# Batch 0's B and C loaded eight tokens to a partition, scaled and transposed in that layout

## The chip, the cores and the metric

The kernel runs on one core of a Trainium2 chip. The metric is the device time of one execution in microseconds (us). Engines are named as the profile names them: PE (matrix products; PEld are its weight loads), DVE (vector), ACT (activations and copies), POOL, and SP, whose queue here issues every transfer between memory and the chip.

## The reference, cut to what matters

A Mamba-2 scan over chunks feeds a low-rank mixer with a channel network. All sizes are small: 4 batches, 8 heads, 768 tokens, 32 values and 16 states per head.

```python
log_a = np.log(np.clip(a, 1e-06, 1.0))
for c in range(nc):                              # chunks of 32 tokens
    xc, Bc, Cc = (x[:, :, sl], B[:, :, sl], C[:, :, sl])
    cum = np.cumsum(log_a[:, :, sl], axis=-1)
    L = np.exp(cum[:, :, :, None] - cum[:, :, None, :]) * causal
    y_intra = ((Cc @ Bc^T) * L) @ xc
    y_inter = (Cc @ state) * np.exp(cum)[..., None]
    y[:, :, sl] = y_intra + y_inter
    state = np.exp(sum(la)) * state + (Bc * np.exp(cum[..., -1:] - cum)[..., None])^T @ xc
...
# y, with heads side by side: X (4, 768, 256)
h = (X.transpose(0, 2, 1) @ U) @ V               # over all 768 tokens, rank 32
u = X + h.transpose(0, 2, 1)
out = u + np.maximum(u @ w_ch1, 0.0) @ w_ch2
```

The four weight arrays arrive as 64-bit floats and are made into 32-bit ones on the chip.

## The kernel before

The kernel takes tokens in chunks of 64. Twelve *pairs* k = 0 to 11 (three to a batch) each cover 256 tokens: two blocks of 128 tokens, or four chunks. Instead of the reference's L it scales B by exp(-sum) and C by exp(+sum), where the sum of log a runs from the middle of each chunk; the array F holds both factors, by tokens.

Everything stands in an order written out by hand: LOADS names the loads issued before anything else, and PLAN is a list of steps that the function `follow` turns into instructions. Each engine takes its instructions strictly in that order. The letters that matter here, k being the pair:

- `b`k.part, `x`k.block, `B`, `X`, `L`: loads of B (two parts, 0 and 2), C (part 1) and x. All go through `begin` (L184) into SP's queue. `Z`/`z` load V and U, `W`/`w` the channel weights.
- `A`, `K`: `decays` and `keep`, the factors F and the decay between chunks.
- `P` (and `Q` for a part): `prep`, DVE scales a pair's B and C by F into BC, by tokens (tokens on partitions).
- `T` (and `V` for one block): `turning` (L478 to L491), PE transposes BC so that states lie on partitions, and ACT (or DVE) copies the result into T and into Cm (C once for even and once for odd heads).
- `g`: `gram` (L509), C times B for all chunks; `m`, `M`: `mask` on DVE; `s`: `state` (L541), B times x; `u`: `update`, DVE carries the state through the chunks, then POOL makes Sm (L567).
- `i`, `j`: `inter` in two halves (L611), `n`: `intra` (L633), `y`: copies of the output (L646), `t`, `O`: transposes of it by tokens (L654).
- `c`: conversion of a piece of the 64-bit weights (DVE and ACT, L415 to L422); `v`: `spread`, V for the mixer (L820, L824); `R`: `refine`, splits of the weights.
- `p`, `q`: the mixer's projection on U (L681, L689); `a`: its product with V added to yT (L699); `U`: the first product of the channel network for batch 0 (L727, with ACT's L744); `d`: the second one; `S`, `f`, `e`, `h` do the same in three parts for batches 1 to 3.
- `F`: products with the identity that write nothing used, to keep PE busy (L137).

Batch 0's mixer needs all of batch 0's scan, pairs 0 to 2, since `p` sums over all tokens. The scan of pair 3 and part of 4 runs in among it. From the first `U` on PE has large products to fill it.

The head of the two lists reads so (LOADS, then the start of PLAN):

```python
'b0.0 b0.1 b0.2 x0.0 x0.1 b1.0 b1.1 b1.2 '
'x1.1 F2.0 A0 Q0.1 x1.0 Q0.0 F3.1 b2.2 A1 Q0.2 V0.1.1 Q1.2 V0.0.0 K0 Q1.1 g0 m0 Q1.0 s0 V1.1.2 '
'M0 n0 u0 V1.0.2 b3.0 F1.1 Q2.1 s1 u1 i0 g1 m1 F3.0 M1 b2.0 Q2.0 b2.1 Q2.2 F1.0 j0 y0 Z0 V2.0.2 '
```

A B load of one block is 128 partitions x 8 heads x 16 floats, 1024 runs of 64 bytes. A C load covers a pair with two neighbouring tokens to a partition, 1024 runs of 128 bytes; an x load has 1024 runs of 128 bytes as well.

Of the kernel before, what the change touches and what calls it, by code (L numbers as in the profile page):

```python
# [10 lines left out]
FP32 = mybir.dt.float32  # L11
INT32 = mybir.dt.int32
# [4 lines left out]
PLAIN = 2  # L17
TAGS = {(2, 1): "yyy", (3, 0): "yyy", (3, 1): "yyy"}
# [16 lines left out]
    'b0.0 b0.1 b0.2 x0.0 x0.1 b1.0 b1.1 b1.2 ')  # L35
PLAN = (
    'x1.1 F2.0 A0 Q0.1 x1.0 Q0.0 F3.1 b2.2 A1 Q0.2 V0.1.1 Q1.2 V0.0.0 K0 Q1.1 g0 m0 Q1.0 s0 V1.1.2 '
    'M0 n0 u0 V1.0.2 b3.0 F1.1 Q2.1 s1 u1 i0 g1 m1 F3.0 M1 b2.0 Q2.0 b2.1 Q2.2 F1.0 j0 y0 Z0 V2.0.2 '
    'V2.1.3 n1 i1 g2 z0 c0 c0 x2.0 x2.1 s2 b3.1 m2 j1 y1 O0.0 u2 b3.2 P3 M2 T3 T3 W0 c1 x3.1 W1 '
    'b4.0 i2 n2 g3 x3.0 c0 c2 c2 M3 j2 y2 m3 t1 O2.1 s3 v0 x4.1 c1 u3 b4.1 c2 c1 p0 n3 i3 b4.2 P4 '  # L40
    'b5.2 b5.0 q0 j3 W2 W3 W4 T4 T4 b5.1 a0.0 a0.1 w5 c3 c3 c3 x4.0 U0.0.0 P5 U0.0.1 y3 U0.1.1 R0 '
    'B6 t3 X5 g4 m4 T5 M4 T5 c5 c5 U0.1.0 c5 X6 U0.1.3 c4 c4 s4 u4 w6 w7 w8 U0.0.3 P6 U0.0.2 c6 '
    'U0.0.6 s5 c4 U0.1.7 c6 U0.1.2 u5 R0 R2 U0.1.6 n4 s6 L7 i4 g5 c6 R4 j4 y4 u6 T6 T6 m5 R2 R1 '
    'U0.0.4 M5 U0.1.4 n5 i5 L8 g6 c7 c7 c9 c9 j5 P7 T7 T7 M6 c7 t4 y5 U0.0.7 c8 U0.0.5 t5 m6 n6 R3 '
    'c9 P8 c8 p1 R7 g7 m7 L9 i6 M7 T8 T8 c8 q1 d0.0.2.0 d0.0.2.1 U0.1.5 a1.1 R1 d0.0.2.2 d0.0.2.3 '
    'a1.0 d0.0.1.0 R3 d0.0.1.1 d0.0.1.2 d0.0.0.0 d0.0.0.1 S1.0 f1.0.0 R7 d0.0.0.2 f1.0.1 d0.0.0.3 '
    'e1.0.0 h1.0.0 R5 d0.0.1.3 f1.0.6 R6 e1.0.1 d0.1.0.0 f1.0.7 P9 d0.1.0.1 h1.0.1 e1.0.6 d0.1.0.2 '
    'L10 R6 h1.0.6 e1.0.7 s7 u7 h1.0.7 f1.0.3 f1.0.2 d0.1.0.3 e1.0.2 d0.1.1.0 P10 h1.0.2 e1.0.3 '
    'h1.0.3 d0.1.2.0 f1.0.4 d0.1.1.1 R4 R4 f1.0.5 d0.1.1.2 d0.1.1.3 e1.0.4 e1.0.5 d0.1.2.1 d0.1.2.2 '
    'h1.0.4 h1.0.5 R6 d0.1.2.3 s8 j6 g8 y6 u8 s9 m8 n7 i7 S1.1 f1.1.0 f1.1.2 j7 y7 u9 M8 t6 R5 '  # L50
    'e1.1.0 h1.1.0 n8 i8 T9 T9 t7 R5 d1.0.1.0 d1.0.1.1 d1.0.1.2 d1.0.0.0 d1.0.0.1 d1.0.0.2 d1.0.0.3 '
    'e1.1.2 R7 f1.1.3 d1.0.0.4 d1.0.0.5 d1.0.1.3 j8 y8 s10 d1.0.2.0 e1.1.3 h1.1.2 h1.1.3 d1.0.1.4 '
    'f1.1.4 d1.0.1.5 f1.1.5 d1.0.2.1 d1.0.2.2 d1.0.2.3 u10 L11 e1.1.4 e1.1.5 h1.1.4 h1.1.5 t8 '
    'd1.0.2.4 f1.1.1 d1.0.2.5 f1.1.6 e1.1.1 h1.1.1 p2 f1.1.7 q2 e1.1.6 d1.1.1.0 e1.1.7 d1.1.0.0 '
    'd1.1.0.1 d1.1.0.2 h1.1.6 h1.1.7 a2.0 S2.0 P11 d1.1.1.1 d1.1.1.2 d1.1.1.3 d1.1.0.3 d1.1.2.0 '
    'd1.1.2.1 d1.1.2.2 d1.1.2.3 d1.1.0.4 d1.1.0.5 d1.1.2.4 d1.1.2.5 d1.1.1.4 d1.1.1.5 T10 g9 m9 T10 '
    'T11 T11 M9 i9 n9 g10 m10 M10 j9 y9 s11 u11 i10 g11 m11 M11 n10 f2.0.4 a2.1 f2.0.3 f2.0.2 '
    'e2.0.4 h2.0.4 e2.0.3 e2.0.2 f2.0.7 f2.0.6 h2.0.2 h2.0.3 f2.0.0 f2.0.1 e2.0.0 e2.0.7 e2.0.1 '
    'h2.0.0 h2.0.1 j10 y10 t9 e2.0.6 h2.0.6 h2.0.7 f2.0.5 i11 n11 e2.0.5 h2.0.5 d2.0.1.0 d2.0.0.0 '
    'd2.0.0.1 d2.0.0.2 d2.0.0.3 d2.0.1.1 d2.0.1.2 d2.0.1.3 S2.1 d2.0.0.4 d2.0.0.5 d2.0.1.4 d2.0.1.5 '  # L60
    'f2.1.1 d2.0.2.0 d2.0.2.1 d2.0.2.2 d2.0.2.3 f2.1.0 d2.0.2.4 d2.0.2.5 j11 y11 t10 f2.1.3 e2.1.0 '
    'f2.1.2 h2.1.0 t11 e2.1.3 e2.1.1 h2.1.1 e2.1.2 h2.1.2 h2.1.3 f2.1.4 p3 e2.1.4 f2.1.5 f2.1.6 '
    'h2.1.4 e2.1.5 h2.1.5 q3 f2.1.7 e2.1.6 d2.1.0.0 e2.1.7 d2.1.2.0 d2.1.2.1 d2.1.2.2 h2.1.6 h2.1.7 '
    'd2.1.2.3 a3.0 S3.0 d2.1.0.1 d2.1.0.2 d2.1.0.3 a3.1 d2.1.2.4 d2.1.2.5 f3.0.1 f3.0.0 d2.1.0.4 '
    'f3.0.6 e3.0.0 h3.0.0 e3.0.1 d2.1.1.0 f3.0.3 d2.1.1.1 d2.1.1.2 d2.1.1.3 h3.0.1 f3.0.2 d2.1.1.4 '
    'e3.0.6 h3.0.6 e3.0.2 h3.0.2 d2.1.1.5 e3.0.3 h3.0.3 d2.1.0.5 f3.0.4 f3.0.5 f3.0.7 e3.0.4 h3.0.4 '
    'e3.0.5 d3.0.2.0 e3.0.7 d3.0.1.0 d3.0.2.1 d3.0.2.2 h3.0.5 d3.0.1.1 d3.0.1.2 S3.1 f3.1.4 f3.1.1 '
    'h3.0.7 d3.0.2.3 d3.0.1.3 f3.1.0 e3.1.4 h3.1.4 d3.0.2.4 e3.1.0 d3.0.2.5 e3.1.1 f3.1.5 d3.0.0.0 '
    'f3.1.2 d3.0.0.1 d3.0.0.2 d3.0.0.3 e3.1.2 h3.1.0 h3.1.1 f3.1.3 e3.1.5 h3.1.5 h3.1.2 d3.0.0.4 '
    'f3.1.6 e3.1.3 h3.1.3 d3.0.0.5 f3.1.7 d3.0.1.4 d3.0.1.5 e3.1.6 h3.1.6 e3.1.7 h3.1.7 d3.1.1.0 '  # L70
    'd3.1.1.1 d3.1.1.2 d3.1.1.3 d3.1.2.0 d3.1.2.1 d3.1.1.4 d3.1.1.5 d3.1.2.2 d3.1.2.3 d3.1.0.0 '
    'd3.1.0.1 d3.1.0.2 d3.1.0.3 d3.1.2.4 d3.1.2.5 d3.1.0.4 d3.1.0.5 ')
# [3 lines left out]
def kernel(  # L76
# [70 lines left out]
    class Kept:  # L147
# [6 lines left out]
        def __getattr__(self, name):  # L154
# [120 lines left out]

    def load(k):
        if k < NB * NPR:
            load_bc(k)
            load_x(k)
# [3 lines left out]
                 z=lambda n: load_u())  # L283
# [166 lines left out]
    st = {}  # L450
    settled = const.tile([P, 1], FP32)
# [145 lines left out]
    def inter(k, part):  # L597
# [7 lines left out]
        for c in range(2):  # L605
            for r in range(4):
# [240 lines left out]
    scans = dict(P=prep, T=turned, g=gram, s=state, m=lambda k: mask(k, (0, 1)),  # L847
# [58 lines left out]
```

## Time and profile before

| | |
|---|---|
| median of 3 runs | 229.58 us (227.76 to 229.64) |
| the profiled execution's own time | 230.14 us |
| its span in the profile | 228.4 us |
| PE busy | 215.8 us (94%) |
| DVE, ACT, POOL busy | 157.7, 114.4, 14.1 us |
| transfers issued by SP, KB each | 24 of B (64), 12 of C (128), 24 of x (128), 24 of the output (128), 14 of weights |

The span is what the engines' records cover; the device time has 1.74 us more around it. PE's busy time includes stages in which it works on small products that wait for one another, so its share alone does not say where it sets the pace; that is read stage by stage, from the idle time before an instruction and from the chain of waits that ended last.

### The profile page before, as it was taken

To read this page: it belongs to the slowest core of one execution; us is meant where nothing else is said; L and a number is where in the kernel's file an instruction comes from. 1 tells how busy PE (TensorE), PEld (TensorE's weight loads), DVE (VectorE), ACT (ScalarE), POOL (GpSimd) and SP (SyncE) were. 2 spreads that over 40 slices of the span, in tenths; PEclk is the share of its full clock that TensorE was granted. 3 is DMA by queue.
4 is the path that set the end of the run, shared out by engine and by line. 5 is a ranking of instruction groups with operands and counts; after the bars stand their busy time and mean duration, and the time that the engine had idled before them with its cause. 6 is when DMAs were issued, how large, how long until landed. Compare 5 with 4: busy or idle time off the path is not lost.

```text
span 228.4 us, 7003 instructions
## 1 busy us (share of the span) xinstructions
PE 215.8 (94%) x3008; PEld 183.2 (80%) x3008; DVE 157.7 (69%) x331; ACT 114.4 (50%) x260; POOL 14.1 (6%) x37
## 2 busy tenths in 40 slices
PE   7798588999999999999999999999999999999993
PEld 4466455655578899898899899897998999999993
DVE  4586688889999857869736775767447973774821
ACT  3336453886798155542634540566336545655410
POOL 3020010011100000201201000100000000000000
PEclk9999799999999999999999999999999999999999
DMA  6987977588771501701001801000010000100011
GB/s 88 127 96 132 168 110 235 136 115 279 97 95 24 97 3 46 114 3 49 3 3 46 119 0 69 6 3 0 4 46 26 0 0 26 46 0 26 24 46 46
DMA packets 69518, 14.56 MB, mean 64 GB/s; under 512 B 63792, under 2 KB 67696, under 8 KB 69488
## 3 DMA queue, kind: packets, MB, share of 16 engines
q1 hardware_dynamic: 69488, 14.13, 33.4%
q8 instruction: 23, 0.38, 0.8%
q14 instruction: 7, 0.06, 0.1%
HBM read 10.98 MB, written 3.15 MB: 62 GB/s over the span
## 4 chain that ended last, share of the span: by engine, by line
PE 84%; SPq 8%; DVE 3%; DMA 2%; issue 1%; ACT 0%; DVEq 0%
PE x L727 30%; PE z L727 23%; PE y L727 12%; SPq L184 8%; PE y L633 3%; PE y L611 3%; PE w L478 2%; DMA bc<-in_B_dram 2%; PE x L509 2%; PE w L654 2%; PE w L541 2%; PE z L509 1%; PE w L681 1%; DVE words L158 1%; DVE S L158 1%
## 5 line engine op out<-in xcount | busy, mean ns | idle before, releaser
L158 DVE SCALAR_TENSOR_TENSOR words<-words 128x768 fp32r<-128x768 f32 (+6 forms) x44 | 35.1, 816 | 1.7 <-ACT words L415 0.4
L727 PE MATMUL z<-u,w 128*128 128x384 f32 x144 | 34.0, 350 | 0.0
L727 PE MATMUL x<-u,w 128*128 128x384 f32 x144 | 33.2, 348 | 0.0
L732 ACT ACTIVATE x<-x 128x384 f32<-128x384 f32 (+1 forms) x30 | 13.6, 452 | 25.2 <-PE x L727 25.1
L727 PEld LDWEIGHTS z<-u,w 128*128 128x128 f32 x144 | 24.6, 188 | 1.3 <-DVE words L158 0.2
L727 PEld LDWEIGHTS x<-u,w 128*128 128x128 f32 x144 | 24.0, 188 | 1.3 <-ACT x L732 0.6
L158 DVE SCALAR_TENSOR_TENSOR words<-x,words 128x384 fp32r<-128x384 f32 x24 | 13.3, 556 | 16.4 <-ACT words L761 13.7
L727 PE MATMUL x<-w2c,words 128*128 128x256 f32 x112 | 22.5, 338 | 0.0
L732 ACT ACTIVATE z<-z 128x384 f32<-128x384 f32 (+1 forms) x27 | 12.5, 463 | 14.2 <-PE z L727 13.6
L727 PEld LDWEIGHTS x<-w2c,words 128*128 128x128 f32 x112 | 18.2, 189 | 1.3
L727 PE MATMUL y<-w,words 128*128 128x256 f32 x144 | 19.1, 282 | 0.0
L727 PEld LDWEIGHTS y<-w,words 128*128 128x128 f32 x144 | 18.5, 188 | 0.3 <-DVE ytok L158 0.3
L158 DVE SCALAR_TENSOR_TENSOR words<-z,words 128x384 fp32r<-128x384 f32 x24 | 13.2, 552 | 5.7 <-ACT words L761 5.7
L761 ACT ACTIVATE words<-x 128x384 fp32r<-128x384 f32 x24 | 11.6, 490 | 6.3 <-PE x L727 6.2
L761 ACT ACTIVATE words<-z 128x384 fp32r<-128x384 f32 x24 | 11.6, 491 | 4.9 <-PE z L727 4.8
L567 POOL TENSOR_TENSOR Sm<-S,own 128x256 f32<-128x256 f32 (+1 forms) x12 | 7.8, 654 | 88.0 <-DVE S L158 58.3
L158 DVE SCALAR_TENSOR_TENSOR S<-S,kept,w 128x64 f32<-128x64 f32 x40 | 11.2, 280 | 2.7 <-PE w L541 0.9
L611 PE MATMUL y<-T,Sm 32*64 32x64 f32 x352 | 12.4, 246 | 0.4 <-POOL Sm L567 0.3
L727 PE MATMUL x<-w,words 128*128 128x256 f32 x96 | 12.6, 282 | 0.0
L509 PE MATMUL x<-Cm,T 32*64 32x128 f32 x192 | 11.8, 316 | 0.9 <-ACT Cm L488 0.9
L158 DVE TENSOR_TENSOR BC<-bc,F 128x512 f32<-128x512 f32 (+2 forms) x18 | 9.0, 508 | 5.0 <-DMA bc<-in_B_dram 3.7
L646 ACT COPY yT<-y 128x256 f32<-128x256 f32 x24 | 7.8, 382 | 8.6 <-PE y L611 8.4
(147 smaller groups left out, 403.6 us busy)
## 6 DMA issues: line engine op xcount, KB each, us to landing
words<-in_moe_w_ch_dram SPq DMA_DIRECT2D x7, 512.0 KB, 5.9
x<-in_x_dram SPq DMA_DIRECT2D x24, 128.0 KB, 3.8
out_dram<-ytok SPq DMA_DIRECT2D x24, 128.0 KB, 1.7
bc<-in_B_dram SPq DMA_DIRECT2D x24, 64.0 KB, 3.7
bc<-in_C_dram SPq DMA_DIRECT2D x12, 128.0 KB, 4.0
words<-in_moe_w_ch_dram SPq DMA_DIRECT2D x2, 256.0 KB, 5.0
words<-in_moe_V_dram SPq DMA_DIRECT2D x4, 48.0 KB, 1.9
words<-in_moe_U_dram SPq DMA_DIRECT2D x1, 192.0 KB, 4.4
```

The lines of the kernel that those rows point to most:

```text
L158: self.last = call(*args, **kwargs)
L184: op = nc.sync.dma_start(**kwargs)
L478: nc.tensor.transpose(out=tp[:, i, v], in_=s["BC"][:, i, c + v].rearrange("p h n -> p (h n)"), identity=ident)
L509: nc.tensor.matmul(out=g[r][cols, c], lhsT=s["T"][rows, 0, c, cols], rhs=s["Cm"][rows, :, :, ts(2 * c + p, Q)].rearrange("r v t i -> r v i ...
L541: nc.tensor.matmul(out=s["A"][p][ts(r, Q), v], lhsT=s["BC"][half, 0, v, 2 * r:2 * r + 2].rearrange("p h n -> p (h n)"), rhs=x_sb[k][half, ...
L567: nc.gpsimd.tensor_tensor(out=s["Sm"][:, sl], in0=s["S"][:, sl].rearrange("p i (s d) -> p i s d", s=2), in1=own2[:, b, 4 * q + sl.start:4 ...
L611: product = nc.tensor.matmul(out=y[p][ts(r % 2, H), r // 2, c], lhsT=own[ts(r, Q)], rhs=s["T"][ts(r, Q), 1, :, ts(2 * c + p, Q)].rearrange ...
L633: product = nc.tensor.matmul(out=y[p][ts(i, Q), n, c], lhsT=x_sb[k][half, c, h], rhs=s["M"][half, h // 2, c, h % 2], start=fresh(k, p, [i] ...
L646: nc.scalar.copy(out=yp[:, :, :, p], in_=st[k]["y"][p])
L727: nc.tensor.matmul(out=t, lhsT=lhsT, rhs=rhs, start=start, stop=True, skip_group_check=True)
L732: nc.scalar.activation(t, t, AF.Copy, scale=1.0 + EPS)
L761: nc.scalar.activation(gs[j, m // 2][0][:, m % 2], t, AF.Relu, scale=NEAR)
```

## The change

For batch 0 alone (WIDE = 1):

1. B and C of the whole batch come as one load each (`k0.0`, `k0.1`), with eight neighbouring tokens to a partition: 96 partitions x 8 heads x 128 floats, 768 runs of 512 bytes. The nine loads `b0.*`, `b1.*`, `b2.*` go. One more load brings batch 0's `a` in the same layout (96 partitions, 768 runs of 32 bytes), and it stands first; the load of all of `a` follows fourth (`o0`).
2. The factors for batch 0 are made in that layout (`J`): clamp, logarithm, a running sum over the eight tokens on DVE (`tensor_tensor_scan`), one product with a matrix that adds the other partitions of the same 64-token chunk and one with the identity, two exponentials into F8. The matrix is built on POOL by four selections and a subtraction. The logarithms of all batches (`I`) and `decays` for batches 1 to 3 come later.
3. `E` scales half of the eight tokens of B or C (DVE, 96 x 512), `G` transposes those four 96 x 128 pieces on PE, `Y` copies them into the batch-wide tile Tall with tokens in their natural order, `N` makes Cm.
4. `H` transposes the scaled B back by tokens for `state`, two products and a copy for each pair.
5. Products that read T and Cm of batch 0 take 64 neighbouring columns where they took two interleaved runs of 32; the y of a batch comes out accordingly in natural order.
6. LOADS and PLAN are written anew from end to end: the same steps for the other batches stand in another order.

```diff
+WIDE = 1
 LOADS = (
-    'b0.0 b0.1 b0.2 x0.0 x0.1 b1.0 b1.1 b1.2 ')
+    'k0.0 k0.1 o0 x0.0 x0.1 x1.0 ')
 PLAN = (
+    'F2.1 x2.1 Z0 b3.1 F3.2 J0 E0.0.1 W0 F3.1 E0.1.0 I0 G0.0.1.3 Y0.0.1.0 Y0.0.1.1 G0.1.0.2 '
+    'Y0.1.0.0 Y0.1.0.1 E0.1.1 G0.1.1.2 Y0.1.1.1 Y0.1.1.0 N0.0 A0 E0.0.0 G0.0.0.3 Y0.0.0.0 Y0.0.0.1 '
+    'K0 F1.2 g0 m0 M0 H0.0 s0 u0 N0.1 n0 H2.0 z0 c0 H1.0 i0 g1 M1 m1 j0 A1 x1.1 s1 u1 y0 c1 c1 g2 '
+    'M2 n1 F2.0 i1 c0 b3.2 m2 b3.0 P3 x2.0 s2 j1 y1 u2 T3 c0 T3 c1 x3.0 O0.0 i2 W1 n2 c2 g3 M3 j2 '
+    'y2 m3 c2 t1 O2.1 p0 x3.1 s3 v0 u3 c2 x4.0 q0 n3 b5.0 i3 b4.2 b4.0 b5.1 b4.1 P4 a0.0 T4 T4 b5.2 '
+    'P5 x4.1 R0 W2 W3 W4 w5 X5 w6 w7 U0.0.1 a0.1 T5 j3 y3 c3 c3 g4 m4 T5 t3 U0.0.0 B6 M4 c3 U0.1.1 '
...
+    for b in range(WIDE):
+        nc.sync.dma_start(out=runs[:, 0, b].rearrange("p (h t) -> p h t", t=TB),
+                          in_=a[b].rearrange("h (p t) -> p h t", t=TB))
...
+    def load_wide(b, i):
+        raws[b, i] = spare()
+        begin(out=raws[b, i].rearrange("p (h f) -> p h f", h=NH),
+              in_=(B, C)[i][b].rearrange("h (p t) n -> p h (t n)", t=TB))
...
+    select(0, ones, [[-groups, PW // groups], [0, groups]], 0, 1)
...
+    nc.gpsimd.tensor_tensor(out=octet[0], in0=octet[0], in1=octet[1], op=ALU.subtract)
...
+    def runs_of():
+        flat = [runs[:, v].rearrange("p b f -> p (b f)") for v in range(4)]
+        vector.tensor_scalar(out=flat[1], in0=flat[0], scalar1=1e-6, scalar2=1.0, op0=ALU.max,
+                             op1=ALU.min)
+        nc.scalar.activation(flat[2], flat[1], AF.Ln)
+        vector.tensor_tensor_scan(
+            out=flat[3], data0=follows, data1=flat[2],
+            initial=0.0, op0=ALU.mult, op1=ALU.add)
...
+        for i in range(2):
+            nc.scalar.activation(F8[:, i], d, AF.Exp, scale=(-1.0, 1.0)[i])
...
+    def prep_wide(b, i, v):
+        half = ts(v, TB // 2)
+        vector.tensor_tensor(
+            out=out, in0=raws[b, i].rearrange("p (h t n) -> p t h n", h=NH, n=N)[:, half],
+            in1=F8[:, i, b].rearrange("p (h t) -> p t h", t=TB)[:, half, :, None].to_broadcast(
+                out.shape), op=ALU.mult)
...
+    def place_wide(b, i, v, part):
+        qs = (slice(0, 1), slice(1, NPR), slice(0, NPR))[part]
+        out = Tall[:, i, qs].rearrange("p q c (m t) -> p (q c m) t", t=TB)[:, :, ts(v, TB // 2)]
+        nc.scalar.copy(
+            out=out, in_=turned_raw[b, i, v][:, :, qs.start * Q:qs.stop * Q].rearrange(
+                "p t m -> p m t"))
...
+    def back_wide(k, tag):
+        for c in range(2):
+            nc.tensor.transpose(out=t[:, c], in_=s["T"][:, 0, c], identity=ident)
+        nc.scalar.copy(out=s["BC"][:, 0].rearrange("p c h n -> p c (h n)"), in_=t)
...
-                        rhs=s["Cm"][rows, :, :, ts(2 * c + p, Q)].rearrange("r v t i -> r v i t"),
+                        rhs=piece(s["Cm"], k, rows, 2 * c + p),
```

## The prediction

> **What bounds the kernel now.** I read the page first, then the busy time by stages, cut where the first product of the channel network starts (38.4 us) and where the last ends (224.8).
>
> ```profile
> span 228.4 us, 7003 instructions
> PE 215.8 (94%) x3008; PEld 183.2 (80%) x3008; DVE 157.7 (69%) x331; ACT 114.4 (50%) x260; POOL 14.1 (6%) x37
> PEclk9999799999999999999999999999999999999999
> ```
> ```profile
> 0.00:38.40 38.40, 29.99 (x734) 20.64 (x734) 25.44 (x81) 16.35 (x45) 5.58 (x21) 0.96 0.89 141
> 38.40:80.00 41.60, 41.10 (x625) 28.06 (x626) 38.12 (x83) 30.00 (x65) 3.10 (x5) 1.00 0.61 116
> 80.00:224.80 144.80, 144.66 (x1651) 134.53 (x1649) 93.72 (x168) 68.01 (x152) 5.40 (x11) 1.00 0.12 28
> 224.80:228.40 3.60, 0.00 (x0) 0.00 (x0) 0.42 (x1) 0.00 (x0) 0.00 (x0) 0.87 0.21 73
> ```
>
> The columns are the stretch, its length, busy us of PE, PEld, DVE, ACT and POOL, the granted clock, DMA share and GB/s. From 38.4 us PE is never without work (185.8 of 186.4 us), and until 80 us DVE is nearly as full (38.1 of 41.6). So the end is the start of the first large product, plus the PE work behind it, plus a 3.6 us tail. Only ahead of 38.4 is time to be had, and there I read the chain of waits in order of time, then PE's largest idle stretch in the timeline:
>
> ```profile
> 15.60 0.42 SPq L184
> 16.07 0.54 SPq L184
> 16.66 0.58 SPq L184
> 17.28 2.57 SPq L184
> 19.89 4.67 DMA bc<-in_B_dram
> 24.69 0.70 DVE BC L158
> 25.53 0.63 PE w L478 x4
> ```
> ```profile
> 25.53 0.63 PE L478 MATMUL w<-ident,BC 128*128 128x128 f32 x4 [3.08 <-DVE BC L158]
> ```
>
> The chain is SP's queue from 0.8 to 19.9 us, one issue behind another, and then 4.7 us until pair 3's last B load lands. Pair 3's `prep` starts only then (24.69), PE has stood still for 3.1 us, and the clock is 0.66 from 25 to 30 us. Behind it pair 3's `gram` starts at 27.84, the projection at 32.88, the first product at 38.41.
>
> **What the change does to the loads.** Nine loads go (6 x 64 KB of B, 3 x 128 KB of C, 1024 runs each) and three come. In the trace the first loads of 1024 runs land 0.90 us apart (3.92 to 15.58 us, 13 steps), whether of B, C or x: 9 x 0.90 = 8.1 us. The new ones: 768 packets of 512 bytes at 27.8 ns (mean of the 192 in the load of `a`) on 16 engines are 1.33 us each, and 768 of 32 bytes at about the 12.4 ns of 64-byte ones 0.6, together 3.3. So the loads behind come about 4.8 us sooner. By these, from first packets at 1.8 us: `a` 3.0, B 4.4, C 5.7, all of `a` 6.0, x then every 0.9. Pair 3's last B load, now about the 17th, lands by 17 to 19 us, also if one load is held up as U's was (3.1 us for 192 KB). Its new cover is ample: it is wanted at 21.4 (below).
>
> **The new head, step by step.** What must come before the first `gram` is longer now.
> - POOL ends `mine` at 3.55 (as before); four selections (0.29), a subtraction (0.33) and two fills: 5.45. DVE's scan waits for the last fill. No row shows a scan: 0.19 (64x64 `causal`) to 0.52 (128x352 reduction); I take 0.3, by the size: 5.8.
> - Two fp32 products 64 columns wide: between 0.26 (L369) and 0.87 (L365, PE not yet at full clock), 0.6: 6.45. Exponentials 0.25 each (L391 0.24): 6.95, the first at 6.75.
> - DVE's four `E` in the form 128x512 (0.69, start to start 0.60), with the clamp of all logarithms between the second and third: done 7.45, 8.05, 9.0, 9.6.
> - Four transposes for each (0.63). ACT has the logarithm of all ahead of its copies: 8.55 to 8.9; then six copies `Y` at 0.27 start to start, 10.5; two Cm, 0.84, 11.35; F and the last T copy: `gram` of pair 0 at 11.9. Before it starts at 9.95: 1.95 us are lost here.
> - Then the steps of before at their rows: gram 0.95, H0 and its copy 0.75, `state` 0.55, four links of S at 0.30, Sm 0.62: 15.9. Gram of pair 1 at 16.15, its four masks to 18.3, gram of pair 2 at 18.55 (before 19.44), its masks to 21.4. There `P3` follows at once: 22.0. S of pair 2 and Sm: 23.5; `inter`, `intra` 24.8; gram of pair 3 25.95 (before 28.98); output copies and transposes; projection 27.7 to 28.75 (before 33.7).
> - Behind the projection now stand `s3` and `spread`, which before stood ahead of it: state 0.45, `spread` 1.4, its four copies on ACT to 31.75, then `ps` on ACT and DVE to 32.6, `a0.0` 0.45, the sum into yT on DVE (behind `P4`) 33.8. First product at 33.9: 4.5 us sooner.
>
> **What is given back.** (a) Behind the first product there is more PE work: `j3` (16 products, 0.43 to 0.49 in rows of L611) and the two of `a0.1` (0.19 each) stood ahead of it: +0.8. The rest of batch 0 to 3 is the same products. (b) Directly behind it come `a0.1`, `g4` and masks rather than twelve large products; gram 4 waits for DVE's second sum: 0.4. (c) Pair 8's load waits for DVE's last weight split, some 4.0 us of DVE work before `P8`; three such loads in a row took 4.8 to 5.4 us from release to landing (rows at 43, 62, 72 us). DVE stands 0 to 0.9 us there; PE has between nothing and 1.9 us in hand: 0.3. (d) The copies `Y` read PSUM in steps of 96 floats. ACT's copy with a stepped output (L646) takes 0.382 against 0.372 without; DVE's `same`, which reads in steps of 32, takes 1.7 times a plain row per element. ACT's rate is 0.84 ns per element ((0.586-0.372)/256), so seven copies ahead of gram cost 0 to +0.8: I take 0.2, by ACT's own row. (e) POOL's selections and F8 cost nothing beyond what is counted; DVE's work by steps changes from 148.8 to 148.6 us, and ACT's +1.7 fall where ACT has 22 of 38 us idle.
>
> [...]
>
> Sum: -4.5 + 0.8 + 0.4 + 0.3 + 0.2 = -2.8 us. The span becomes 225.6 and that execution's time 227.3; its own time stood 0.56 above the median, so against the median 229.58 I say **226.8**.
>
> **The rivals.**
> 1. *Nothing is given back* (chance 0.17): PE stays full, the copies cost their plain rows, and the head's steps without a row (scan, the two products, the fills) come at their lower ends, 0.6 us less. -4.5 + 0.8 - 0.6 = -4.3: 225.3. For: PE lost nothing from 38.4 to 80 us before, though by step sums DVE runs up to 0.8 us behind PE there. Against: by the same sums it is 1.1 behind now.
> 2. *DVE takes over* (0.15): from first product to +42 us PE and DVE have equal work in both kernels, and a head that is 4.5 us shorter leaves DVE fewer idle us (13 before, 8.7 now). If DVE needs 5% more than the step sums, 2.1 of the 2.8 go: 228.9. For: 92% busy. Against: it managed before, with the same work.
> 3. *The change does not speed the loads* (0.06): if the 512-byte packets pass as U's 768 did (3.1 us a load), B lands at 6.1 and C at 9.2, `E` of C starts 1.8 us late and all behind it: 228.6. If U's rate holds by bytes (192 KB), C lands at 15.6 and the kernel is slower by 5 us. Against: the 192 packets of `a` passed in 0.66 us.
> 4. *Slower* (0.10): the seven `Y` copies ahead of the first gram, one after another on ACT. If each read across PSUM steps costs 0.41 us more (0.78 instead of 0.37) the 2.8 us are used up; at 1.1 us each it is 7 x 0.73 = 5.1 in place of the 0.2 counted: 231.7. For: no ACT row has such a read. Against: ACT works element by element in all its rows here.
>
> **How the numbers follow.** The forecast has 0.52. Its own range is 225.4 to 228.4, about three quarters of it below 227.3, which is faster by over 1% (1% is about what a measurement of this kernel tells from no change): 0.38 faster, 0.14 within. Rival 1: faster 0.17. Rival 2: 0.13 within, 0.02 slower. Rival 3: 0.05 and 0.01. Rival 4: 0.01 and 0.09. Together faster 0.55, within 0.33, slower 0.12. The range runs from a little below rival 1, 224.8, to 229.9, which leaves out rival 4 and some of the tails.
>
> **What would show it.** The profile after should have: SP's queue no longer in the chain between 10 and 20 us; `gram` of pair 0 at 11.9, of pair 3 at 25; no PE idle over 2 us ahead of the first product and no clock under 0.9 there; the copies of L588 at 0.3 to 0.4 us; the first product of L847 at 33 to 35; PE full behind it to about 222, with a hole of at most 1 us near 76. I am wrong if the first product comes after 36.5, if L588 takes over 0.7, or if PE shows more than 2 us of idle between 35 and 80.

## The result and the profile after

| | before | after |
|---|---|---|
| median of 6 runs each | 229.61 us (227.70 to 229.80) | 237.36 us (235.37 to 239.65) |
| ratio, 95% interval | | 1.034 (1.027 to 1.041) |
| profiled execution, its span | 230.14, 228.4 | 235.37, 233.5 |
| first large product starts | 38.41 | 40.59 (forecast 33.9) |
| from there to the end of the last product | 186.4 | 189.8 |

The changed kernel is slower by 3.4%. Its profiled execution is the shortest of the six, with a mean clock of 0.985 where the other five have 0.957 to 0.964, so it shows 5.1 of the 7.8 us, and where the others lost the rest no trace shows. Its page:

```profile
span 233.5 us, 7022 instructions
PE 217.8 (93%) x3020; PEld 184.3 (79%) x3020; DVE 159.5 (68%) x324; ACT 114.9 (49%) x264; POOL 15.3 (7%) x44
PEclk9769999999999999999999999999999999999999
PE 81%; DVE 9%; issue 4%; DMA 2%; ACT 1%; SPq 1%; POOL 1%; DVEq 0%; POOLq 0%
```

SP's queue, 7.7% of the chain before, is down to 1%, as meant. In its place stands "issue", time in which an engine waited for nothing that the profile shows. The busy time by stages of after, cut at the first large product and 42 us behind it (columns as in the prediction):

```profile
0.00:40.59 40.59, 31.03 (x733) 21.64 (x733) 26.52 (x74) 16.57 (x47) 7.88 (x28) 0.92 0.77 138
40.59:82.59 42.00, 40.98 (x633) 27.77 (x633) 38.71 (x83) 30.62 (x64) 3.10 (x6) 1.00 0.43 87
82.59:230.40 147.81, 145.79 (x1658) 134.87 (x1656) 93.89 (x169) 67.72 (x153) 4.27 (x10) 1.00 0.17 34
```

The same for before, in one stretch:

```profile
38.41:224.85 186.44, 185.76 (x2274) 162.59 (x2274) 131.87 (x251) 98.00 (x216) 8.51 (x16) 1.00 0.23 48
```

So the 5.1 us of span are 2.2 ahead of the first product, 1.0 of PE work moved behind it (40.98 + 145.79 against 185.76), 2.4 of PE idle behind it (3.0 against 0.7), less 0.45 at the very end. PE's rows with an idle time put down to "issue" in the timeline of after:

```profile
24.23 0.41 PE L753 MATMUL y<-M,x 64*32 64x64 f32 x19 [1.17 <-issue]
29.48 0.65 PE L753 MATMUL y<-M,x 64*32 64x64 f32 x39 [0.69 <-issue]
35.51 0.35 PE L661 MATMUL w<-x,BC 64*32 64x64 f32 x16 [0.96 <-issue]
...
150.19 0.35 PE L661 MATMUL w<-x,BC 64*32 64x64 f32 x16 [0.50 <-issue]
153.64 0.50 PE L731 MATMUL y<-Tall,Sm 32*64 32x64 f32 x16 [1.16 <-issue]
```

The stops fall in the middle of groups of equal products whose operands are long there. If PE's instructions (products and weight loads) are numbered by their starts, these stops stand ahead of numbers 706, 962, 1218, 4546 and 4802: always 194 and a multiple of 256. From one stop to the next PE runs some 127 products and as many weight loads, which the busy time by stages shows (the counts in brackets behind the first two busy times):

```profile
20.12:24.22 4.10, 2.77 (x127) 2.05 (x128) 3.35 (x11) 2.01 (x6) 0.61 (x1) 1.00 0.75 96
24.22:29.47 5.25, 4.11 (x126) 2.96 (x126) 4.87 (x13) 2.64 (x8) 0.94 (x2) 1.00 0.96 162
```

The page's third part has a queue of its own for this, `q8 instruction: 23, 0.38`: 23 transfers of 16 KB, as many whole blocks of 256 as PE's 6040 instructions fill. Set beside the boundaries, from the trace (us):

| block entered | fetch began (late by) | fetch ended | next block's first instruction (after that) | stop |
|---|---|---|---|---|
| after, 20.13 | 22.00 (1.87) | 22.96 | 24.23 (1.27) | 1.17 |
| after, 24.23 | 27.02 (2.79) | 27.98 | 29.48 (1.51) | 0.69 |
| after, 29.48 | 33.08 (3.60) | 34.09 | 35.51 (1.42) | 0.96 |
| after, 150.19 | 151.30 (1.11) | 152.38 | 153.64 (1.27) | 1.16 |
| before, 15.15 | 17.09 (1.94) | 18.73 | 20.04 (1.31) | none |
| before, 31.98 | 34.82 (2.84) | 35.78 | 37.20 (1.43) | 0.31 |

**Theory 1**: at these places a block of 256 instructions is fetched only after the one ahead of it has been entered (1.11 to 3.60 us after, in the table), later where loads are in flight (1.11 us in the row of after whose block has a DMA share of 0.02, 1.87 to 3.60 in the three with 0.62 to 0.96), and the block's first instruction follows some 1.3 us after the fetch's end (1.27 to 1.51). At the first large product of after it was otherwise: a fetch began at 40.58 us, 1.1 us ahead of instruction 1474. The new head has its small products closer together and therefore runs into that limit. The rivals: **theory 2**, order and dependencies alone (the head makes DVE late, DVE makes the rest late); **theory 3**, the half clock from 8.7 to 15.6 us; **theory 4**, the wide loads, which landed later than forecast, with the load of all of `a` behind them.

### The profile page after: what moved, and what is told of

It is laid out like the page before. It is cut to its first block, busy times and chain, and to the rows that moved or that the text cites. A ratio compares the mean times of both kernels' runs of the same rounds, so it can differ in the third digit from the quotient of the medians.

```text
span 233.5 us, 7022 instructions
## 1 busy us (share of the span) xinstructions
PE 217.8 (93%) x3020; PEld 184.3 (79%) x3020; DVE 159.5 (68%) x324; ACT 114.9 (49%) x264; POOL 15.3 (7%) x44
## 4 chain that ended last, share of the span: by engine, by line
PE 81%; DVE 9%; issue 4%; DMA 2%; ACT 1%; SPq 1%; POOL 1%; DVEq 0%; POOLq 0%
PE x L847 26%; PE z L847 21%; PE y L847 12%; DVE words L160 5%; PE y L731 4%; PE y L753 3%; DMA a_sb<-in_a_dram 2%; PE x L629 2%; DVE S L160 2%; PE w L545 2%; PE w L774 2%; PE w L661 2%; PE w L801 2%; PE z L629 1%; PE w L809 1%
## 5 line engine op out<-in xcount | busy, mean ns | idle before, releaser
L847 PE MATMUL x<-u,w 128*128 128x384 f32 x144 | 33.9, 350 | 0.0
L847 PE MATMUL z<-u,w 128*128 128x384 f32 x144 | 32.4, 344 | 0.0
L731 PE MATMUL y<-Tall,Sm 32*64 32x64 f32 x352 | 12.0, 236 | 2.0 <-issue 1.3
L731 PEld LDWEIGHTS y<-Tall,Sm 32*64 32x64 f32 x352 | 8.5, 131 | 6.1 <-issue 3.3
L847 PE MATMUL x<-w,words 128*128 128x256 f32 x96 | 13.1, 285 | 0.0
L753 PE MATMUL y<-M,x 64*32 64x64 f32 x768 | 11.2, 224 | 1.9 <-issue 1.9
```

The lines of the kernel that those rows point to most:

```text
L731: product = nc.tensor.matmul(out=y[p][ts(r % 2, H), r // 2, c], lhsT=own[ts(r, Q)], rhs=piece(s["T"], k, ts(r, Q), 2 * c + p)[:, 1], start ...
L753: product = nc.tensor.matmul(out=y[p][ts(i, Q), n, c], lhsT=x_sb[k][half, c, h], rhs=s["M"][half, h // 2, c, h % 2], start=fresh(k, p, [i] ...
L847: nc.tensor.matmul(out=t, lhsT=lhsT, rhs=rhs, start=start, stop=True, skip_group_check=True)
```

## The experiments

Times are medians; "before" is the kernel before on the same chip. Stops are PE's idle times at boundaries of 256 ahead of the first large product, from the one profiled execution.

| run | time | before | ratio (95%) | first product | stops |
|---|---|---|---|---|---|
| r1 new head, old tail | 233.25 | 229.1 | 1.011 to 1.023 | 40.83 | 2.13 |
| r2 old head, new tail | 232.86 | 229.1 | 1.010 to 1.022 | 38.01 | 0 |
| r3 before, moved by 192 | 236.71 | 229.1 | 1.026 to 1.040 | 43.54 | 2.39 |
| r4 before, moved by 256 | 233.91 | 229.1 | 1.015 to 1.026 | 41.27 | 0.54 |
| r5 W2 to W4 later | 236.79 | 229.3 | 1.010 to 1.034 | 41.09 | 3.67 |
| r6 more warm products | 234.57 | 229.3 | 1.015 to 1.027 | 39.29 | 2.53 |
| r7 logarithms later | 235.41 | 229.3 | 1.018 to 1.032 | 41.54 | 2.80 |
| r8 r1 + r6 + r7 | 235.94 | 229.3 | 1.015 to 1.034 | 44.75 | 4.56 |
| r9 r6, loads spread | 236.06 | 228.3 | 1.028 to 1.039 | 37.95 | 2.21 |
| r10 r9 with old tail | 234.94 | 228.3 | 1.024 to 1.035 | 42.21 | 3.60 |
| r11 r6, loads even | 235.58 | 228.7 | 1.022 to 1.037 | 38.84 | 3.86 |
| r12 r11 with old tail | 234.59 | 228.7 | 1.020 to 1.031 | 41.16 | 1.75 |
| r14 r6, W2 to W4 behind first product | 236.58 | 230.0 | 1.013 to 1.046 | 36.89 | 1.24 |
| r15 candidate | 232.84 | 229.9 | 1.006 to 1.015 | 40.53 | 1.55 |
| r16 candidate, boundaries as before | 230.06 | 229.9 | 1.000 to 1.007 | 39.33 | 1.72 |
| r17 r16, W1 later | 229.06 | 229.2 | 0.995 to 1.002 | 38.83 | 1.74 |
| r18 r17, logarithms later | 230.65 | 229.2 | 1.001 to 1.009 | 38.81 | 0.90 |

### Head or tail (r1, r2)

PLAN is cut at `P4`; each run takes the words up to there from one kernel and those behind from the other. In r1:

```diff
-'... P4 a0.0 T4 T4 b5.2 P5 x4.1 R0 W2 W3 W4 w5 X5 w6 w7 U0.0.1 a0.1 T5 j3 y3 c3 c3 g4 ...'
+'... P4 b5.2 x4.1 j3 W2 W3 W4 T4 T4 a0.0 a0.1 w5 c3 c3 c3 U0.0.0 P5 U0.0.1 y3 U0.1.1 ...'
```

> The changed kernel up to P4, and from there the words of the kernel before (its order behind the first large product, with j3 and a0.1 ahead of it again). Theory 1: TensorE's instructions arrive in blocks of 256 (16 KB each in the trace); the next block is fetched only once a block has been entered, and its first instruction runs no sooner than 1.3 us after the fetch has ended. In the changed kernel that stops PE for 1.17 + 0.69 + 0.96 us ahead of the first product and 0.50 + 1.16 us at 149 to 154 us. The new head keeps its stops, the old tail has its small products spread otherwise: first product at about 41.4 us (40.7 and the 0.8 of j3 and a0.1), 186.4 to 187.5 us from there to the last product, time 233.0 to 234.5. Theory 2: the blocks cost nothing by themselves, what is lost behind the first product comes from the head (DVE arrives there late and stays late): 188.5 us or more behind the first product also with the old order, time 235 or more.

> The kernel before (nine loads for batch 0's B and C) up to P4, and from there the words of the changed kernel. Theory 1 (blocks of 256 instructions): first product at 37.5 to 38.5 us, and behind it the new order's bunched small products near 147 to 152 us stop PE again for 1 to 1.7 us: 188 to 189.5 us behind the first product, time 231 to 232.5. Theory 2 (the loss behind the first product comes from the new head): 186.5 to 187 us behind it, time 229 to 230.

r1 is 4.1 us above the kernel before and r2 3.8; together 7.9, and the change cost 7.8. Both halves lose on their own: behind the first product r1 needs 187.7 us with the old order, and r2 189.6 with the old head. So the head does not make the rest late, and theory 2 falls in that form. r2 missed its figures on the long side (231 to 232.5 us, 188 to 189.5 of them behind the first product). Of its 3.2 us over the kernel before there, 1.3 are PE work and 1.1 a stop at a boundary; the rest is waiting for other engines, which the new order has too. r2's stop, where no load is near (timeline, one row):

```profile
151.03 0.34 PE L611 MATMUL y<-T,Sm 32*64 32x64 f32 x3 [1.10 <-issue]
```

### The place of the boundaries (r3, r4)

```diff
-    warm(3, "x")
+    count = bank("x", 4 * P)
+    for i in range(49):       # 65 in r4
+        nc.tensor.matmul(out=count[:32, :32], lhsT=ident[:32, :32], rhs=ident[:32, :32],
+                         start=True, stop=True)
```

> The kernel before with its first warm product (4 of PE's instructions) replaced by 49 products of 32 x 32 x 32 (196 instructions) in the same gap at 1.4 to 2.9 us, so that every later boundary of 256 instructions falls 192 instructions earlier in the program; nothing else differs. Theory 1: the boundaries now fall into the dense stretches of small products: PE stands 1.2 to 1.8 us near 58 us, 0.8 to 1.2 near 109 and about 0.6 near 149, together 2.3 to 3.4: time 231.8 to 233. Theory 2 (the place of the boundaries doesn't matter): 229.2 to 230.2, as before.

> As the run beside it, but with 65 such products (260 instructions), so that the boundaries fall on the same instructions as in the kernel before, one block later. Both theories: as the kernel before within 0.6 us (229.0 to 230.2), with PE never idle over 0.4 us behind the first product. If it is as slow as the run with 192, the small products themselves cost the time and not the boundaries.

My products cost more than I allowed, 0.11 us each (49 in 5.43 us): they end at 6.9 us in r3 and 8.6 in r4, so both heads begin late and both runs missed their figures. They still tell the theories apart. r4 begins 1.7 us later than r3 and reaches its first product 2.3 us sooner; at the end it is 2.8 us ahead. The rows of r3, then of r4 (lines are 3 higher than before):

```profile
26.16 0.35 PE L544 MATMUL w<-x,BC 64*32 64x64 f32 x17 [1.37 <-issue]
32.58 0.37 PE L512 MATMUL z<-Cm,T 32*64 32x128 f32 x1 [0.75 <-issue]
39.21 0.41 PE L684 MATMUL w<-ytok,UV 128*32 128x128 f32 x3 [0.27 <-issue]
```
```profile
26.39 0.29 PE L512 MATMUL z<-Cm,T 32*64 32x128 f32 x1 [0.54 <-issue]
```

The same kernel stops at other instructions when only their numbers change (962, 1218, 1474 again). The clock differs as well: in r3 it is half from 27.9 to 38.2 us, behind the stop at 26.16, and in r4 it stays full, so the 2.8 us are stops and clock together. The further stops expected near 58 and 109 us did not come (0.2 at most); why not, no row here shows.

### A block by itself (r13)

```diff
     follow(PLAN)
+    room = [bank(tag, 4 * P) for tag in "xzwy"]
+    for i in range(768):
+        rows = ts(i % 4, Q)
+        nc.tensor.matmul(out=room[i // 64 % 4][rows, ts(i // 4 % 8, 64)], lhsT=ident[rows, rows],
+                         rhs=ident[rows, :64], start=True, stop=True, skip_group_check=True)
+    for n in range(8):
+        t = words_of(w1f[0])
+        nc.sync.dma_start(out=t..., in_=w13[:, :, ts(1, 2 * quarter)])
```

> The kernel before, and behind its last instructions 768 small products on TensorE (32 x 32 by 32 x 64, of four row groups in turn, 3072 of its instructions, 12 blocks of 256) that wait for nothing, and 8 loads of 512 KB that start behind the last output: the disputed cost by itself. Theory 1: a block takes 3.0 to 3.5 us with no load in flight, 1.0 to 1.5 us of them a stop at its end, and 4.5 to 6.5 us while the loads run, with the fetch beginning 2 us or more after the block was entered. The rival (blocks cost nothing, the stops in the head have another cause): 256 instructions every 1.9 to 2.3 us throughout, no stops at the boundaries.

The busy time by stages, cut at block boundaries; the first with loads in flight, the others without:

```profile
225.94:232.41 6.47, 2.00 (x130) 1.83 (x128) 0.00 (x0) 0.00 (x0) 0.00 (x0) 0.92 0.93 291
242.61:246.34 3.73, 1.99 (x128) 1.83 (x128) 0.00 (x0) 0.00 (x0) 0.00 (x0) 1.00 0.02 4
246.34:250.07 3.73, 1.99 (x128) 1.83 (x128) 0.00 (x0) 0.00 (x0) 0.00 (x0) 1.00 0.02 4
```

From 243 to 256 us the only traffic is four fetches (slices of the DMA view for that window, and its queue):

```profile
DMA  0020000000000010000000000200000000000200
q8 instruction: 4, 0.07, 2.2%
```

So a block has a price of its own. 256 instructions that wait for nothing take 3.73 us, more than the 3.0 to 3.5 expected, of which PE works 1.99 and stands 1.74, the same for seven blocks in a row; the fetch begins 1.0 to 1.5 us after the block is entered, lasts 0.9 to 1.4, and the next instruction follows 1.2 to 1.5 us later. Beside 512 KB loads the fetch begins 4.0 and 4.25 us late, and a block takes 6.47 us (twice, the second time with PE at half clock). A single block can pass sooner where its successor's fetch began early: in the kernel before, the block entered at 143.5 us took 2.7 us, since the fetch for the next one had begun at 142.9, before its own first instruction.

### The loads beside the fetch (r5, r9 to r12, r14)

Each run moves loads alone, by another place in PLAN and a capital or small letter that holds the load until DVE's last instruction ahead of the word. r14's edit:

```diff
-'... A1 x1.1 s1 u1 ... b3.2 m2 b3.0 P3 x2.0 s2 ... c1 x3.0 O0.0 i2 W1 ... O2.1 p0 x3.1 ... x4.0 q0 n3 b5.0 i3 b4.2 b4.0 b5.1 b4.1 P4 a0.0 T4 T4 b5.2 P5 x4.1 R0 W2 W3 W4 w5 ...'
+'... A1 x1.1 b3.2 b3.0 x2.0 W1 s1 u1 ... m2 P3 X3 s2 ... c1 B4 O0.0 i2 ... M3 B5 ... O2.1 p0 ... q0 n3 i3 P4 a0.0 T4 T4 P5 w2 W3 W4 X4 R0 w5 ...'
```

r5 and r11 read, in the same form:

```diff
 # r5
-'... O2.1 p0 x3.1 s3 v0 u3 c2 x4.0 q0 n3 b5.0 i3 b4.2 b4.0 b5.1 b4.1 P4 a0.0 T4 T4 b5.2 P5 x4.1 R0 W2 W3 W4 w5 ...'
+'... O2.1 x3.1 x4.0 b5.0 b4.2 b4.0 b5.1 b4.1 b5.2 x4.1 w2 w3 w4 p0 s3 v0 u3 c2 q0 n3 i3 P4 a0.0 T4 T4 P5 R0 w5 ...'
 # r11 (r9: W1 X3 behind P3 and u2, then B4, w2, w3, B5, w4)
+'... x1.1 b3.2 b3.0 x2.0 W1 s1 u1 w2 y0 c1 c1 g2 M2 X3 ... P3 B4 ... T3 c1 B5 ... M3 w3 ... u3 w4 c2 ... P5 X4 R0 w5 ...'
```

> The changed kernel with the three 512 KB loads W2 to W4 held until DVE has copied the last tokens' output of batch 0 (some 33 us; they were issued from 26.5 us on and landed at 31.9 to 34.7), the smaller loads that stood behind them ahead. Theory 1 (a fetch of PE's instructions waits behind the loads): the fetch that began 3.6 us after PE had entered its block (29.48 to 33.08) begins within 1.5 us, the stop of 0.96 us at 34.55 is gone or under 0.3, the first large product comes at 39.6 to 40.0 instead of 40.6, time 0.5 to 1.2 us shorter: 236.2 to 236.9. The rival: a fetch takes its time whatever the loads do; then the stop stays at 0.8 to 1.1 us and the time is the same or longer, since W2 to W4 come later.

r5: the fetch that began 3.60 us late now begins 0.88 late, and the stop at 35 us is gone. But the next fetch, now beside W2 to W4, begins 4.08 late, and PE stands 1.96 there. The profile puts the end of this wait down to DVE's second `prep` of pair 4, done at 40.33, 0.26 us before PE goes on at 40.59; the fetch ended at 39.30, 1.3 us before. So this row alone does not tell the two apart. The first product came no sooner (41.09), and four executions of 233.4 to 237.9 us, the profiled one the longest, do not show whether time was won.

> The changed kernel with the two more warm products (as in the run r6, 234.57 us, first large product at 39.3, stops of 0.36, 1.93 and 0.24 us ahead of it) and with the loads that are not wanted soon issued later, each held until DVE has passed a point of the head: x of pair 3 at the S chain of pair 2, B and C of pair 4 some 1.5 us on, W2 at 30, W3 at 32, B and C of pair 5 at 33, W4 at 36, x of pair 4 behind the first product; no operation is added or taken away. Theory 1: the fetches at 20, 26 and 32 us begin within 1.3 us of PE's entering the block instead of 2.5, 3.7 and 3.0, the stop at the third boundary (1.93) falls to 0.3 to 0.8, the first product comes at 37.3 to 38.5, time 232.6 to 233.8. The rivals: the stops stay, since small products are issued faster than blocks can come in any case (1.5 us or more, first product at 39 to 39.6, 234 to 235); or a load now comes too late for the instruction that wants it, and PE waits for that instead (235 or more).

> The same head with the order of the kernel before behind P4 (the run r1 without these edits: 233.25 us). If the head's gain and the old tail's add up: 1.5 to 2.5 us less than r1, 230.8 to 231.8 us, still above the kernel before (229.3); if the spread loads gain nothing, 232.0 to 233.5.

> As r9 (more warm products, loads held until DVE has passed a point), with the points moved so that nothing comes late and the transfers lie evenly between 20 and 40 us: W2 at 21.7, x of pair 3 at 23, B and C of pair 4 at 24.5, of pair 5 at 28.5, W3 at 30, W4 at 34, x of pair 4 behind the first product; the order behind P4 is that of the changed kernel. Theory 1: no fetch begins later than 2 us after its block was entered, the stops ahead of the first product stay under 1.5 us together without the last one at #450, the first product comes at 37.5 to 38.5 (r9: 37.95), and r9's wait for B and C of pair 5 (1.33 us) is gone: 1 to 2 us below r9's 236.06, 234.0 to 235.0, with the stops of about 1.7 and 0.5 at 148 to 153 us still there. The rival: each load put anywhere holds up the fetch beside it, the stops only move: first product 38.5 to 40, time 235 to 236.

> The same with the order of the kernel before behind P4 (as r10, 234.94, and r1, 233.25). Theory 1: the stop of 1.98 at the sixth boundary of r10 falls under 1 us and with it the half clock from 38.7 us: first product at 39 to 40, 187 to 187.8 us behind it, time 231.0 to 232.5. The rival: as r10 and r1, 233 to 235.

r9 took the late fetches down to 1.2 to 1.7 us and brought the first product to 37.95, as expected, but lost it again: B and C of pair 5 landed at 40.3 (1.33 us of PE waiting), and a stop of 1.70 at 153 us was followed by 3.4 us of half clock in a stretch where PE sets the end; its second rival, a load that comes too late, held. r10, r11 and r12 came out between 234.6 and 235.6: in all four runs with the 1.5 MB of W2 to W4 ahead of the first product, the stops there still add up to 1.75 to 3.86 us. Here the rival was right.

> As r11, but W2 to W4 (1.5 MB) are issued only behind the first large product, so that from 20 to 38 us only x of pair 3 and B and C of pairs 4 and 5 are loaded (0.75 MB). What is looked at is the first product, not the end: the pieces of W2 to W4 come late for DVE, and 2 us or more are lost behind it. Theory 1: stops ahead of the first product under 2 us together (r11: 3.86, r6: 2.5 and more), first product at 36.3 to 37.5. The rival (the stops come whatever the loads do): 3 us or more of stops, first product at 38 to 39.5.

With W2 to W4 out of the head, the fetches from 18 us on begin 0.6 to 1.2 us late, and from there to the first product no boundary stops PE; the one stop left, and the first product:

```profile
18.21 0.32 PE L629 MATMUL z<-Cmall,Tall 32*64 32x128 f32 x1 [1.25 <-issue]
...
36.89 1.56 PE L847 MATMUL z<-yT,w1f 128*128 128x384 f32 x4
```

That is 3.7 us ahead of the changed kernel and 1.5 ahead of the kernel before. Its time is no better (236.58): in the 42 us behind it PE works 39.02 us and DVE 35.37, against 40.98 and 38.71 in after, with a clock of 0.96 against 1.00. The expectation put such a loss down to weights that come late for DVE; how much of it they are, no row here shows.

### Clock and a's load (r6, r7, r8)

```diff
-'... b3.1 F3.2 J0 E0.0.1 W0 F3.1 E0.1.0 ...'
+'... b3.1 F3.2 F2.0 J0 E0.0.1 W0 F3.1 F2.1 E0.1.0 ...'
```

> The changed kernel with two more warm products in PE's two gaps of 0.95 us (5.2 to 6.2) and 0.7 us (7.4 to 8.1). Theory 3 (the clock): PE is idle 1.6 us of the 3.4 us ahead of 8.74, and the 6.8 us at half clock behind that come from it. With the gaps filled the clock stays full, the products of keep take 0.45 instead of 0.74 to 0.90 us, gram of pair 0 starts at 12.8 to 13.1 instead of 13.87, the first large product 0.6 to 1.0 us sooner, time 235.8 to 236.8, and the runs lie closer together (they had clocks from 0.957 to 0.985). The rival: ACT's copies and DVE's chain set the head, and what PE gains ahead is taken back at the boundaries of instruction blocks: first product within 0.3 us of 40.6, time within 0.5.

The keep products of after at half clock, then of r6, with pair 0's first gram row in each:

```profile
12.24 0.74 PE L449 MATMUL z<-la,high 128*128 128x160 f32 x2
...
13.87 0.48 PE L629 MATMUL x<-Cmall,Tall 32*64 32x128 f32 x2
```
```profile
10.64 0.43 PE L449 MATMUL z<-la,high 128*128 128x160 f32 x2
...
11.75 0.32 PE L629 MATMUL x<-Cmall,Tall 32*64 32x128 f32 x2 [0.18 <-ACT Tall L588]
...
22.28 0.65 PE L753 MATMUL y<-M,x 64*32 64x64 f32 x23 [1.93 <-issue]
```

Gram starts 2.1 us sooner, but the stop ahead of instruction 706 grows from 1.17 to 1.93, and the first product is only 1.3 us sooner. That is more than the expectation gave (0.6 to 1.0; 234.57 us against 235.8 to 236.8), and the rival's 0.3 us is exceeded; but a part was taken back at a boundary, as the rival said. The clock mattered. (r1 and r5 have this part of after unchanged and had gram at 12.57 and 12.68. Their clock records begin at 10.3 and 10.6 us; ahead of that the first four transposes of 96x96 took 0.85 us together, against 0.49 in after at full clock, and from there to 24 us the clock is full. So where the half clock falls differs from one execution to the next.)

> The changed kernel with the logarithms of all batches (I) behind the fourth E instead of between the second and third, so that DVE's third E no longer stands behind the load of all of a (landed 8.07, clamp 8.54 to 9.04). Theory 4 (the wide loads land late and a's load stands in the chain): E's end at 9.7 instead of 10.15, T's copies 0.4 us sooner, gram of pair 0 at 13.4 or so, time 0.3 to 0.6 us shorter. The rival: keep's products, which need these logarithms, come later by as much and gram behind them: no change or 0.3 us longer.

> The new head with the old order behind P4 (233.25 us in the run before) and the two edits of the head: more warm products, and the logarithms behind the fourth E. If both gains of the head hold: 0.9 to 1.5 us shorter, 231.8 to 232.4 us, with the first product at 39.4 to 40.0. If what is won ahead is taken back at the boundaries of PE's instruction blocks: 233 us or more.

```diff
-'... E0.1.0 I0 G0.0.1.3 ... E0.1.1 G0.1.1.2 Y0.1.1.1 Y0.1.1.0 N0.0 A0 E0.0.0 G0.0.0.3 ...'
+'... E0.1.0 G0.0.1.3 ... E0.1.1 E0.0.0 I0 G0.1.1.2 Y0.1.1.1 Y0.1.1.0 N0.0 A0 G0.0.0.3 ...'
```

With this edit gram comes later each time it can be compared: 12.94 in r7 against 12.68 in r5, 12.25 in r8 against 11.75 in r6, 13.74 in r18 against 13.22 in r17. So the load of all of `a` in DVE's order is no cause, as the rivals of r7 and r18 said. r7's median is still 2 us below that of the changed kernel (1.018 to 1.032 against 1.027 to 1.041, on another chip); its first product came no sooner (41.54), and no run here shows why. r18's median is 1.6 us above r17's, but their profiled executions have the same span (228.6 us, both at full clock): five of r18's twelve executions had a mean clock of 0.985, r17's were all at 0.993 or more. The other half of theory 4, that the wide loads came late, no run takes by itself; in after B had landed (5.71) before DVE wanted it (7.01), and C landed at 7.70, when the `E` ahead of it ended. r8 did not add up (235.94, not 231.8 to 232.4): three stops, 4.56 us, and in its profiled execution (238.31 us, of four from 234.37) half clock from 36.3 to 46.6 us.

### A version that gives the loss back (r15 to r18)

r15: r1's order, r6's warm products, W2 and x of pair 3 behind `P3`, pairs 4 and 5 as in r14, W3 and W4 behind `P4`. r16 in addition puts 59 small products of four row groups in place of the first warm ones, so that behind the head the boundaries fall where they did before. r17 moves W1, and r18 adds r7's edit:

```diff
 # r15, against r1 with r6's words
-'... P3 x2.0 s2 ... x3.0 O0.0 i2 W1 ... P4 b5.2 x4.1 j3 W2 W3 W4 T4 T4 a0.0 a0.1 w5 ...'
+'... P3 w2 X3 s2 ... c1 B4 O0.0 ... M3 B5 ... P4 j3 T4 T4 w3 W4 a0.0 a0.1 X4 w5 ...'
 # r16
-    warm(3, "x")                   # and in PLAN F2.1 ... F3.2 F2.0 by F2.1
+    count = bank("z", 4 * P)
+    for i in range(59):
+        rows = ts(i % 4, Q)
+        nc.tensor.matmul(out=count[rows, ts(i // 4 % 8, 64)], lhsT=ident[rows, rows],
+                         rhs=ident[rows, :64], start=True, stop=True, skip_group_check=True)
 # r17
-'... x1.1 b3.2 b3.0 x2.0 W1 s1 u1 ... P3 w2 X3 s2 ...'
+'... x1.1 b3.2 b3.0 x2.0 s1 u1 ... P3 w1 X3 W2 s2 ...'
```

> The new head with the order of the kernel before behind P4, more warm products, and the loads as r14 showed them to let the blocks through: W2 with x of pair 3 at 24.4 us, B and C of pair 4 at 28, of pair 5 at 30, W3 and W4 at 36.5 behind P4 (the old order converts them from 47 us on), x of pair 4 behind the sum into yT. Theory 1: stops ahead of the first product under 2 us, first product at 37.5 to 38.5 (r14's 36.9 and the 0.8 of j3 and a0.1), 187 to 187.8 us behind it with a stop of about 1 at 151, time 229.5 to 231: as the kernel before or up to 1% slower, 2 to 3.5 us below r1. The rival: W3 and W4 come late for DVE or hold up the fetch at 37 us: 232 to 234.

> As r15, but the first warm products replaced by 59 small ones of four row groups (236 of PE's instructions in the same gap, 1.4 to 5.9 us), so that behind the head each boundary of 256 falls within an instruction or two of where it falls in the kernel before. Theory 1: the stop of about 1 us at 151 falls to at most 0.5, time 0.5 to 1 us below r15: 228.8 to 230.3. The rival: the boundaries in the head move too and stop PE there, or the place in the tail doesn't matter: as r15 or up to 1 us slower.

> As r16, with W1 (256 KB, wanted at 28.6 us, landed 19.7) issued with W2 at 24.4 instead of ahead of it, so that the loads end 0.9 us sooner near 18 us, where PE enters its third block. Theory 1: the fetch behind the second boundary begins some 0.5 us sooner, the stops of 0.54 and 1.18 fall by 0.3 to 0.8 together, time 0.3 to 0.8 us below r16's 230.06. The rival: the stop of 1.18 is a block's own time (3.73 us in r13, 3.82 here) and stays: same as r16 within 0.4.

> As r17, with the logarithms of all batches behind the fourth E (the edit of r7). If E's third instruction stands in the chain of the head behind the load of all of a: 0.3 to 0.5 us sooner at the first gram, and at most 0.3 us of it at the end, since the blocks of the head take their time. The rival: no change or slower by up to 0.3, since keep's products come later.

r15's first product came at 40.53, not 37.5 to 38.5, with half clock from 20.5 to 30.8. r16 is 2.8 us below r15, more than expected; r15's stop of 0.78 at 151 us is gone, but the mean clock of its twelve executions is also higher (0.996 against 0.985), and the runs do not separate numbering from clock. r17 has the time of the kernel before (0.995 to 1.002), with the same wide loads; each against its own kernel before, that is 7.9 us better than the changed kernel. Its page, and what is left ahead of its first product:

```profile
span 228.6 us, 7259 instructions
PEclk9999999999999999999999999999999999999999
```
```profile
23.44 0.31 PE L757 MATMUL y<-M,x 64*32 64x64 f32 x6 [1.45 <-issue]
38.83 1.56 PE L851 MATMUL x<-yT,w1f 128*128 128x384 f32 x4
```

That block took 4.10 us, near the 3.73 of a block alone: the stop remained although W1 was moved away, as r17's rival said, though the time fell by 1.0 us, more than either side allowed. None of the versions is measurably faster than the kernel before.

## Why the prediction was wrong, point by point

The forecast was 226.8 us, within 224.8 to 229.9; the result, 237.4, lies outside and on the other side.

**The loads**: right in direction, short in size. `a` landed at 2.89 (forecast 3.0), B at 5.71 (4.4), C at 7.70 (5.7), all of `a` at 8.07 (6.0). The 27.8 ns for a 512-byte packet held until 4 us (27.0 and 28.2 ns); behind, packets took 43 to 47 ns. The step "from 192 packets of `a`" was drawn from a load (1.82 to 2.51 us in before) during which only 104 packets of another began. What the change was for did come: pair 3's last B load landed at 17.91 (forecast 17 to 19, before 24.57), and SP's queue left the chain.

**The head up to gram**: the unseen operations were priced well: scan 0.29 (0.3), E 0.69, the two products done by 6.72 (6.45). Gram started at 13.87 instead of 11.9. The missing 2 us are mostly the half clock from 8.74 us (0.50 up to 13.87): PE was idle for 1.5 of the 3.4 us ahead of it. The prediction had "no clock under 0.9" as a sign but no term for it. With the gaps filled and the clock full (r6) gram came at 11.75, although all of `a` landed late there too (7.46).

**From gram to the first product, forecast 22.0 us, measured 26.7**: this is the step that failed. The prediction added up rows and semaphore waits; that the instructions themselves have to arrive was in no term. Of the 4.7 us, 2.9 arise up to the end of pair 3's gram (30.86; forecast 25.95), where two stops are 1.17 + 0.69 us, and 1.7 behind the projection (33.77; forecast 28.75), where the third stop is 0.96 and DVE's conversions (two rows of `words`, 37.21 in the chain) put 1.1 ahead of `ps`, which the prediction had placed right behind the projection. The stops are thus 2.8 us and not the whole: r14, with one stop of 1.25 us and 3.4 us of half clock, still took 25.1 us from gram to the first product. So the sum was short by some more in its rows, its waits or the clock, and how that divides stays open.

The five blocks from number 194 to 1474 had to pass in some 20 us by the forecast (194 is in pair 0's `state`, which it placed near 14 us; 1474 stands at the first product, 33.9). They took 25.3 us in after and 23.3 in r14. At the pace of r13 five blocks are 5 x 3.73 = 18.7 us with no load in flight, and this head has loads all along. The price was in the profile of before: its block from 15.15 to 20.04 us already ended only 1.31 us behind the fetch, and elsewhere PE waited for other things (3.08 us at 25.53), while the next block came in. With less of that waiting the fetch set the pace.

**Given back**: (a) 0.8, measured 1.0. (b) and (c) 0.7 together: the idle time behind the first product grew by 2.4, of which 1.66 are two stops at 150 and 153 us, in a stretch that the prediction took for the same products in another order. The hole near 76 us did not come. (d) 0.2 for the copies `Y`: right; one takes 0.25 to 0.40 us (L588), two in a row 0.52 to 0.55, so rival 4 fell: no run shows the 0.41 or 0.73 us more for each copy that it reckoned with.

**The rivals**: 1 (nothing given back) and 2 (DVE takes over) fell: DVE's busy time behind the first product is that of before (38.71 of 42 us; 38.52 before). 3 was half right on the landings and wrong on their weight. The slower outcome had a chance of 0.12, from rivals 2, 3 and 4 together, and none of their mechanisms is the one that came.

## What to carry to other kernels

Where TensorE runs many small products, count its instructions as a resource like a queue: 256 of them (64 fp32 products here) took 3.7 us each time in a row of such blocks (r13) and up to 6.5 beside loads, so where a sum of rows lets several blocks in a row pass faster it is likely priced too low. Before a wait is taken away, look whether it hides such a fetch (before's block from 15.15 us ended 1.31 us behind one), and whether PE's idle time that it leaves elsewhere costs the clock (with two gaps filled, r6 had full clock up to its first gram, which came 2.1 us sooner). Try big loads that are not wanted soon where large products run: with W2 to W4 behind the first one (r14), the stops ahead of it were 1.24 us in place of 3.86 (r11), though the time was no better. A rewritten order has to be judged again in places that the change does not name.

## What the runs showed of the hardware that I had not expected

- TensorE's instructions come in transfers of 16 KB, one at a time (23 in after), and its stops stand a multiple of 256 instructions apart. In before's block from 83.56 to 102.66 us, whose products took longer than the fetch (97.96 to 99.22), PE did not stop at the end; in r13's row of blocks with 1.99 us of work each it stood 1.74 us at every one.
- The fetch came later beside loads: counted from the block's first instruction it began 1.0 to 1.5 us late alone (r13), 4.0 and 4.25 beside the 512 KB loads there, up to 5.2 in r8. Why 1 us is left when nothing else is in flight, no run shows.
- Half clock came in stretches of 3.41 (before, from 26.11 us), 6.83 (after, from 8.74) and 10.24 us (r3, 27.9 to 38.2), and not in the same place in each execution of the same head (after against r1 and r5, above). It followed stops of 1.70 (r9) and 1.42 us (r14) near 153 us, but not one of 1.42 us there in r11.
- A small product on one row group that writes one place over and over took 55 ns a row of the trace (r3: 98 in 5.43 us); on four row groups in turn, with other places, it took 29 ns at the same point of the program (r16: 118 in 3.42 us) and 16 ns at full clock (r13: 128 in 1.99 us).
